# A float32 y split per sub-chunk instead of per piece, and three PSUM banks instead of four for the inner product

## The chip, the cores and the metric

The kernel runs on one core of a Trainium2 chip. The metric is device microseconds (us) of one execution, the median of several. The engines are named as the profile names them: PE (matrix engine, with PEld for its weight loads), DVE (vector), ACT (scalar), POOL (GpSimd) and SP (which issues the DMAs).

## The reference, cut to what matters

```python
X = np.fft.rfft(x, axis=1)                 # x: 8 batches x 3136 tokens x 256
y = np.fft.irfft(X * F, n=3136, axis=1)    # F: complex filter, 1569 bins x 256
h = np.maximum(y @ w_in, 0.0)              # w_in: 256 x 1024
conv = sum(conv_w[k] * hp[:, k:k+3136] for k in range(3))   # hp: h padded by one token at both ends
out = (h * sigmoid(conv)) @ w_out          # w_out: 1024 x 256
```

## The kernel before, in words

**Two phases.** The first (up to about 374 us of the span) does the Fourier transform, the filter and most of the way back for all eight batches, through scratch tensors in device memory. The last stage of the way back is left to be done later, in 14 *pieces* per batch: `last_load` fetches 112x2x256 numbers (`br`), `last_stage` multiplies them by a table into one PSUM bank (eight PE rows of L216 in the trace), and `last_out` writes the result into y. The pieces of batch 0 are done at the end of the first phase, those of batches 1 to 7 inside the second.

**Matrix products in three parts.** `mm3` multiplies float32 numbers as two reduced ones: a rounded part (type fp32r, "hi") and the rest ("lo"); hi x hi, hi x lo and lo x hi are added up in PSUM (L177, L178, L179). So each moving operand must first be split: one copy makes hi, one subtraction makes lo. Before the change y is split as it is written: `last_out` has ACT write hi (`hi_act`, L146) and then DVE write lo (`lo_dve`, L149). y thus exists as two tiles of 3138 tokens a batch, for an even and an odd batch.

**The second phase** goes through 448 *steps* m. A step is one (j, f, i): j is a chunk of 896 tokens (28 of them, 16 steps each), f one of 8 groups of 128 hidden channels, i one of the two sub-chunks of 448 tokens. The program writes the work out in software-pipelined order, and each engine runs its instructions in that order. In step m:

- PE: `inner(m)` (six matmuls of 450 columns into a PSUM tile `ps_h`), the matmuls of a piece if the step has one, then `project(m-6)` (12 matmuls of 256 columns for even steps, 9 for odd ones, into the four banks `po`).
- ACT: `relu(m-1)` (L442, in place in PSUM), a scaled copy to the tile t (L444), the sigmoid of `gate(m-2)` (L454), hi of `split_g(m-3)` (L146, tile g).
- DVE: `conv(m-1)` (L449, L450: two taps from `ps_h` added to t), the product of `gate(m-2)` (L455, called mul(m-2) below; it is the last reader of that step's `ps_h`).
- POOL: lo of `split_g(m-3)` (L152).
- After that `last_out` of the step's piece (ACT, then DVE), and at the end of a chunk, in steps 4 and 5 modulo 16, `evacuate`: two DVE copies each (L490) from `po` to the tile `ot`.

The eight PSUM banks of the second phase are four for `ps_h`, shared by `inner` and the pieces, and four for `po`. The steps with m modulo 16 from 3 to 7 get no piece (`AVOID`). The pieces of a batch are spread over the steps in which the y tiles of the batch two before are no longer read: in some stretches every second or third step has one, and then about 16 steps have none.

Of the kernel before, what the change touches and what calls it, by code (L numbers as in the profile page):

```python
# [22 lines left out]
KT = D // 128  # L23
NF = FF // 128
SUB = 448
NSUB = S // SUB
CH = 2 * SUB
NT = CH // 128


def _k1(g, s):
# [93 lines left out]
def tile_fft_filter_gated_ffn(  # L125
# [16 lines left out]
    nc = tc.nc  # L142
    B = x.shape[0]

    def hi_act(dst, src):
        nc.scalar.activation(dst, src, AF.Copy)  # L146

    def lo_dve(dst, src, hi):
        nc.vector.tensor_tensor(out=dst, in0=src, in1=hi.bitcast(F32), op=ALU.subtract)  # L149

    def lo_pool(dst, src, hi):
        nc.gpsimd.tensor_tensor(out=dst, in0=src, in1=hi.bitcast(F32), op=ALU.subtract)  # L152

# [22 lines left out]
    def mm3(ps, wh, wl, rh, rl, start=True, stop=True, **kw):  # L176
        nc.tensor.matmul(ps, lhsT=wh, rhs=rh, start=start, stop=False, **kw)  # L177
        nc.tensor.matmul(ps, lhsT=wh, rhs=rl, start=False, stop=False, **kw)  # L178
        nc.tensor.matmul(ps, lhsT=wl, rhs=rh, start=False, stop=stop, **kw)  # L179
# [4 lines left out]

    wc = ctx.enter_context(tc.tile_pool(name="wc", bufs=1))
    m2_sb = wc.tile([112, N1], F32, name="m2_sb")
    cw = wc.tile([128, 3, NF], F32, name="cw")
    nc.gpsimd.memset(cw[:, 0, 0:1], 0.0)
    nc.scalar.activation(cw[:, 0, 0:1], cw[:, 0, 0:1], AF.Sigmoid)
    wi = [wc.tile([128, KT, FF], F32R, name=f"wi{h}") for h in range(2)]  # L190
# [3 lines left out]
    ys, yps = {}, []  # L194
# [6 lines left out]

    def y_slices(b, sl):
        if sl.start == 0:
            ys[b] = [yps[b % 2].tile([128, KT, S + 2], F32R, name=f"y{h}") for h in range(2)]
            for t in ys[b]:
                nc.gpsimd.memset(t[:, :, 0:1].bitcast(F32), 0.0)
                nc.gpsimd.memset(t[:, :, S + 1:S + 2].bitcast(F32), 0.0)
        return (t[:, :, 1:S + 1].rearrange("p k (a c) -> p k c a", c=N2)[:, :, sl] for t in ys[b])

    def last_stage(b, c, ps):  # L210

        br = lasts[b, c]
        for j in range(2):
            for k in range(KT):
                o = ps[:, (2 * k + j) * N1:(2 * k + j + 1) * N1]
                nc.tensor.matmul(o, lhsT=br[:, j, 128 * k:128 * k + 128], rhs=m2_sb, start=True, stop=True)  # L216
        lasts[b, c] = ps

    def last_out(b, c):
        yh, yl = y_slices(b, slice(c, c + 2))  # L220
        pv = lasts.pop((b, c))[:, 0:4 * N1].rearrange("p (k c a) -> p k c a", c=2, a=N1)
        hi_act(yh, pv)
        lo_dve(yl, pv, yh)

    forward_pools = ExitStack()
    xp = forward_pools.enter_context(tc.tile_pool(name="xp", bufs=2, side="right"))
# [1 line left out]
    with (  # L228
# [125 lines left out]
        def at(i):  # L354
            return divmod(i, NP) if 0 <= i < NP * B else None
# [12 lines left out]
        with tc.manual_schedule(engines=COMPUTE):  # L368
            for i in range(NI):
                f, m = i, i - SKEW  # L370
                if i == done:
                    for _ in wsteps:
                        pass
                    forward_pools.close()
                    yps.append(ctx.enter_context(tc.tile_pool(name="y_even", bufs=1, side="right", reuse_waits="tile")))
                    lp = ctx.enter_context(tc.tile_pool(name="lp", bufs=2, side="right", reuse_waits="tile"))
                if 1 <= i < 4:
                    nc.sync.dma_start(out=s1_sb[:, 4 * i + 12:4 * i + 16], in_=s1[:, 4 * i + 12:4 * i + 16])
                if (bp := at(f + 7)) and i:
                    load("x", *bp)  # L380
                if bp := at(m + 3):
                    load("a", *bp)
                if i == 6:
                    nc.sync.dma_start(out=s2_sb, in_=s2[:, 0:120])
                    nc.sync.dma_start(out=s2s_sb, in_=s2s[:, 0:120])
                    nc.sync.dma_start(out=m2_sb, in_=m2)
                if 12 <= i < 26 and i % 2 == 0:
                    sl = slice((i - 12) // 2 * 4, (i - 12) // 2 * 4 + 4)
                    load_filter(i // 2 - 6)
                    nc.sync.dma_start(out=i1_sb[:, sl], in_=i1[:, sl])  # L390
                if bp := at(m - 2):
                    filt(*bp)
                pt = third(*bp) if (bp := at(m - 4)) else None
                pf = first(*bp) if (bp := at(f - 1)) else None
                if bp := at(m - 1):
                    second(*bp)
                if pt is not None:
                    store("sb", *at(m - 4), pt)
                if pf is not None:
                    store("sa", *at(f - 1), pf)  # L400
                if 3 <= i < 16:
                    next(csteps, None)
                if i == 16:
                    load_weights(0)
                    load_weights(1)
                if i >= 22:
                    next(wsteps, None)
                if 16 <= i < 30 and i % 2 == 0:
                    copy_filter(i // 2 - 8)
                c = 2 * (i - done)  # L410
                if 0 <= c - 4 < N2:
                    last_out(0, c - 4)
                if 0 <= c - 2 < N2:
                    last_stage(0, c - 2, fps.tile([128, 512], F32, name="ps"))
                if 0 <= c < N2:
                    last_load(0, c)


    yps.append(ctx.enter_context(tc.tile_pool(name="y_odd", bufs=1, reuse_waits="tile")))
    wp = ctx.enter_context(tc.tile_pool(name="wp", bufs=2, reuse_waits="tile"))  # L420
    ps_h = ctx.enter_context(tc.tile_pool(name="ps_h", bufs=4, space=bass.MemoryType.PSUM, reuse_waits="tile"))
    ps_o = ctx.enter_context(tc.tile_pool(name="ps_o", bufs=1, space=bass.MemoryType.PSUM, reuse_waits="tile"))

    outv = out.rearrange("b s d -> (b s) d").rearrange("(j t p) d -> j p t d", p=128, t=NT)
    hs, ts, gs, pos = {}, {}, {}, {}

    def at(m):

        return (m // 16, m // 2 % NF, m % 2) if 0 <= m < 16 * (B * S // CH) else None

    def inner(j, f, i):
        ps = ps_h.tile([128, 512], F32, name="ps_h")[:, 0:SUB + 2]
        fs = slice(128 * f, 128 * f + 128)
        b, u = divmod(2 * j + i, NSUB)
        us = slice(u * SUB, u * SUB + SUB + 2)
        for k in range(KT):
            mm3(ps, wi[0][:, k, fs], wi[1][:, k, fs], ys[b][0][:, k, us], ys[b][1][:, k, us], start=k == 0, stop=k == KT - 1)
        hs[j, f, i] = ps

    def relu(j, f, i):  # L440
# [24 lines left out]
    def project(j, f, i):  # L465
        gh, gl = gs[j, f]
        if f == 0 and i == 0:
            pos[j] = [ps_o.tile([128, 512], F32, name=f"po{k}") for k in range(4)], wp.tile([128, NT, D], F32, name="ot")
        po, ot = pos[j]
        tiles = range(4) if i == 0 else range(4, NT)  # L470
        for t in tiles:
# [7 lines left out]
    def evacuate(j, f, i):  # L479
# [16 lines left out]
    NH = 16 * (B * S // CH)  # L496
    pieces = {}
    for b in range(1, B):
        start = ((NSUB * (b - 1) - 1) // 2 + 1) * 16 + (4 if b == 1 else 0)
        stop = NSUB * b // 2 * 16 + NSUB * b % 2  # L500
        free = [m for m in range(start, stop) if m % 16 not in AVOID]
        for c in range(N2 // 2):
            pieces[free[c * (len(free) - 1) // (N2 // 2 - 1)]] = (b, 2 * c)
    with tc.manual_schedule(engines=COMPUTE):
        for m in range(NH + PLAG):
            if m + 4 in pieces:
                last_load(*pieces[m + 4])
            if a := at(m):
                inner(*a)
            if m in pieces:  # L510
                last_stage(*pieces[m], ps_h.tile([128, 512], F32, name="ps_h"))
            if a := at(m - PLAG):
                project(*a)
            if a := at(m - 1):
                relu(*a)
                conv(*a)
            if a := at(m - 2):
                gate(*a)
            if a := at(m - 3):
                split_g(*a)  # L520
            if m in pieces:
                last_out(*pieces[m])
            if a := at(m - PLAG):
                evacuate(*a)

# [43 lines left out]
```

## Time and profile before

| | us |
|---|---|
| median of 3 runs (1563.34 to 1571.38) | 1569.97 |
| the profiled execution | 1563.82 |
| its span | 1562.0 |
| PE / DVE / ACT / POOL busy | 1503.0 / 1280.6 / 1189.7 / 697.6 |
| second phase, 380 to 1549 us: PE / DVE / ACT / POOL busy of 1169.0 | 1163.4 / 997.8 / 1016.6 / 513.9 |

The profiled execution took 1.8 us more than its span, and 6.2 us less than the median. A row of the timeline gives start, duration, engine, source line, output<-inputs, count, and in brackets the idle time before it with what ended it. A row of groups gives the count, then busy us and mean ns of one, then the idle time before it. Matmul rows overlap, so the time between two starts tells how fast PE goes, not the duration.

### The profile page before, as it was taken

To read this page: it belongs to the slowest core of one execution; us is meant where nothing else is said; L and a number is where in the kernel's file an instruction comes from. 1 tells how busy PE (TensorE), PEld (TensorE's weight loads), DVE (VectorE), ACT (ScalarE), POOL (GpSimd) and SP (SyncE) were. 2 spreads that over 40 slices of the span, in tenths; PEclk is the share of its full clock that TensorE was granted. 3 is DMA by queue.
4 is the path that set the end of the run, shared out by engine and by line. 5 is a ranking of instruction groups with operands and counts; after the bars stand their busy time and mean duration, and the time that the engine had idled before them with its cause. 6 is when DMAs were issued, how large, how long until landed. Compare 5 with 4: busy or idle time off the path is not lost.

```text
span 1562.0 us, 26357 instructions
## 1 busy us (share of the span) xinstructions
PE 1503.0 (96%) x9424; PEld 1346.7 (86%) x9424; DVE 1280.6 (82%) x1965; ACT 1189.7 (76%) x2162; POOL 697.6 (45%) x624
## 2 busy tenths in 40 slices
PE   5799989998999999999999999999999999999998
PEld 3466656656999999999999999999999999999998
DVE  0578888888888888888888888888888888888887
ACT  3444444436888888888888888888888888888887
POOL 0356555643444444444444444444444444444444
PEclk9799999999999999999999999999999999999999
DMA  9999999993111011111110111111011110100001
GB/s 306 298 342 350 330 339 343 335 280 105 31 54 48 31 48 48 48 48 48 48 42 28 33 55 48 48 48 48 31 42 48 48 53 25 48 25 25 25 25 48
DMA packets 129397, 166.82 MB, mean 107 GB/s; under 512 B 10906, under 2 KB 87795, under 8 KB 129267
## 3 DMA queue, kind: packets, MB, share of 16 engines
q1 hardware_dynamic: 129267, 165.14, 32.8%
q8 instruction: 75, 1.23, 0.3%
q14 instruction: 55, 0.45, 0.1%
HBM read 88.03 MB, written 77.07 MB: 106 GB/s over the span
## 4 chain that ended last, share of the span: by engine, by line
PE 82%; DMA 12%; DVE 2%; SPq 1%; ACT 1%; issue 1%; POOL 0%; ACTq 0%; POOLq 0%
PE ps_h L178 12%; PE ps_h L179 12%; PE ps_h L177 11%; PE po L475 11%; PE po L477 11%; PE po L476 11%; PE ps_h L216 6%; DMA a<-a_dram 4%; DMA a_dram<-sa 3%; PE pp L328 3%; PE ps L351 2%; PE ps L321 2%; DMA b_dram<-sb 2%; DVE y L149 1%; ACT y L146 1%
## 5 line engine op out<-in xcount | busy, mean ns | idle before, releaser
L152 POOL TENSOR_TENSOR g<-t,g 128x448 fp32r<-128x448 f32 x448 | 517.5, 1155 | 668.2 <-ACT g L146 266.5
L475 PE MATMUL po<-wo,g 128*128 128x256 f32 x1568 | 441.5, 282 | 0.0
L477 PE MATMUL po<-wo,g 128*128 128x256 f32 x1568 | 433.8, 277 | 0.0
L476 PE MATMUL po<-wo,g 128*128 128x256 f32 x1568 | 433.4, 276 | 0.0
L449 DVE SCALAR_TENSOR_TENSOR t<-ps_h,cw,t 128x448 f32<-128x448 f32 x448 | 305.5, 682 | 82.8 <-ACT t L444 71.9
L178 PE MATMUL ps_h<-y,wi 128*128 128x450 f32 x896 | 330.4, 369 | 4.6 <-DVE y L149 4.6
L177 PE MATMUL ps_h<-y,wi 128*128 128x450 f32 x896 | 328.5, 367 | 3.2 <-DVE t L455 1.5
L179 PE MATMUL ps_h<-y,wi 128*128 128x450 f32 x896 | 328.6, 367 | 0.0
L450 DVE SCALAR_TENSOR_TENSOR t<-ps_h,cw,t 128x448 f32<-128x448 f32 x448 | 306.4, 684 | 16.0
L444 ACT ACTIVATE t<-ps_h,cw 128x448 f32<-128x448 f32 x448 | 285.1, 636 | 41.8 <-POOL g L152 0.4
L475 PEld LDWEIGHTS po<-wo,g 128*128 128x128 f32 x1568 | 294.7, 188 | 7.0
L476 PEld LDWEIGHTS po<-wo,g 128*128 128x128 f32 x1568 | 294.3, 188 | 5.7
L477 PEld LDWEIGHTS po<-wo,g 128*128 128x128 f32 x1568 | 294.4, 188 | 0.0
L442 ACT ACTIVATE ps_h<-ps_h 128x450 f32<-128x450 f32 x448 | 251.7, 562 | 31.8 <-PE ps_h L179 27.2
L455 DVE TENSOR_TENSOR t<-ps_h,t 128x448 f32<-128x448 f32 x448 | 275.1, 614 | 0.1
L454 ACT ACTIVATE t<-t 128x448 f32<-128x448 f32 x448 | 255.0, 569 | 12.1 <-DVE t L450 10.9
L146 ACT ACTIVATE g<-t 128x448 fp32r<-128x448 f32 x448 | 254.4, 568 | 0.2 <-DVE t L455 0.2
L344 POOL TENSOR_TENSOR z<-u,v 120x512 f32<-120x512 f32 x112 | 156.8, 1400 | 172.3 <-DVE v L342 162.9
L309 ACT ACTIVATE sb<-ps 112x512 f32<-112x512 f32 x112 | 66.8, 597 | 159.2 <-DMA b_dram<-sb 87.9
L179 PEld LDWEIGHTS ps_h<-y,wi 128*128 128x128 f32 x896 | 168.3, 188 | 13.9
L178 PEld LDWEIGHTS ps_h<-y,wi 128*128 128x128 f32 x896 | 168.3, 188 | 13.6 <-DVE y L149 6.8
L177 PEld LDWEIGHTS ps_h<-y,wi 128*128 128x128 f32 x896 | 169.9, 190 | 11.5 <-DVE t L455 2.6
(51 smaller groups left out, 1474.0 us busy)
## 6 DMA issues: line engine op xcount, KB each, us to landing
x<-in_x SPq DMA_DIRECT2D x112, 224.0 KB, 4.8
a_dram<-sa SPq DMA_DIRECT2D x112, 224.0 KB, 4.5
a<-a_dram SPq DMA_DIRECT2D x112, 224.0 KB, 4.7
b_dram<-sb SPq DMA_DIRECT2D x112, 224.0 KB, 4.5
br<-b_dram SPq DMA_DIRECT2D x112, 224.0 KB, 2.6
out<-ot SPq DMA_DIRECT2D x27, 896.0 KB, 4.1
raw<-in_w_in SPq DMA_DIRECT2D x8, 256.0 KB, 4.6
raw<-in_w_out SPq DMA_DIRECT2D x8, 256.0 KB, 5.6
```

Of the source, the lines that this page charges most:

```text
L146: nc.scalar.activation(dst, src, AF.Copy)
L152: nc.gpsimd.tensor_tensor(out=dst, in0=src, in1=hi.bitcast(F32), op=ALU.subtract)
L177: nc.tensor.matmul(ps, lhsT=wh, rhs=rh, start=start, stop=False, **kw)
L178: nc.tensor.matmul(ps, lhsT=wh, rhs=rl, start=False, stop=False, **kw)
L179: nc.tensor.matmul(ps, lhsT=wl, rhs=rh, start=False, stop=stop, **kw)
L444: nc.scalar.activation(t, h[:, 1:SUB + 1], AF.Copy, scale=cw[:, 1, f:f + 1])
L449: nc.vector.scalar_tensor_tensor(out=t, in0=h[:, 0:SUB], scalar=cw[:, 0, f:f + 1], in1=t, op0=ALU.mult, op1=ALU.add)
L450: nc.vector.scalar_tensor_tensor(out=t, in0=h[:, 2:SUB + 2], scalar=cw[:, 2, f:f + 1], in1=t, op0=ALU.mult, op1=ALU.add)
L455: nc.vector.tensor_mul(t, h[:, 1:SUB + 1], t)
L475: nc.tensor.matmul(o, lhsT=gh[:, sl], rhs=wo[0][:, f], start=first, stop=False, skip_group_check=True)
L476: nc.tensor.matmul(o, lhsT=gh[:, sl], rhs=wo[1][:, f], start=False, stop=False, skip_group_check=True)
L477: nc.tensor.matmul(o, lhsT=gl[:, sl], rhs=wo[0][:, f], start=False, stop=last, skip_group_check=True)
```

## The change

y is kept once, in float32, in a tile `y` for an even and one for an odd batch. `last_out` becomes a single copy: ACT for batch 0, DVE for the others. A new function `window(n)` splits the 450 tokens (448 and one at either side) that sub-chunk n needs: ACT writes hi of 2 x 450 numbers in a partition, POOL writes lo, into tiles `yw` of three buffers. Windows 0 and 1 are made ahead of the loop, later ones at the ends of steps 13 and 15 modulo 16. `inner` reads the window. The inner product has three PSUM banks of its own (`ps_h`), the pieces have one (`ps_l`); `po` keeps its four. Since a batch's y is free once its last window has been made, the pieces of each batch start where those of the last one stopped, and end some steps before the batch itself begins. Three sizes are raised: `cw` is cut from a tile of 6 instead of 3 planes, a window's row holds 464 numbers, a row of `y` 3144; with these the tiles that PE reads in the second phase start at multiples of 64 bytes (by adding up the tile sizes), where most started 32 bytes off.

```diff
-        hi_act(yh, pv)
-        lo_dve(yl, pv, yh)
+        if engine == "act":
+            nc.scalar.activation(y, pv, AF.Copy)
+        else:
+            nc.vector.tensor_copy(y, pv)
...
-    cw = wc.tile([128, 3, NF], F32, name="cw")
+    cw = wc.tile([128, 6, NF], F32, name="cw")[:, 0:3]
...
+    yw = ctx.enter_context(tc.tile_pool(name="yw", bufs=3, reuse_waits="tile"))
-    ps_h = ctx.enter_context(tc.tile_pool(name="ps_h", bufs=4, space=bass.MemoryType.PSUM, reuse_waits="tile"))
+    ps_h = ctx.enter_context(tc.tile_pool(name="ps_h", bufs=3, space=bass.MemoryType.PSUM, reuse_waits="tile"))
+    ps_l = ctx.enter_context(tc.tile_pool(name="ps_l", bufs=1, space=bass.MemoryType.PSUM, reuse_waits="tile"))
...
+    def window(n):
+        b, u = divmod(n, NSUB)
+        src = ys[b][:, :, u * SUB:u * SUB + SUB + 2]
+        wh, wl = (yw.tile([128, KT, WROW], F32R, name=f"yw{h}")[:, :, 0:SUB + 2] for h in range(2))
+        hi_act(wh, src)
+        lo_pool(wl, src, wh)
+        wins[n] = wh, wl
...
-        start = ((NSUB * (b - 1) - 1) // 2 + 1) * 16 + (4 if b == 1 else 0)
-        stop = NSUB * b // 2 * 16 + NSUB * b % 2
+        start = stop if b > 1 else 4
+        stop = NSUB * b // 2 * 16 - 3 + 2 * (NSUB * b % 2)
...
+        for n in range(2):
+            window(n)
...
             if m in pieces:
-                last_out(*pieces[m])
+                last_out(*pieces[m], "dve")
+            if m % 16 in (13, 15):
+                window(2 * (m // 16 + 1) + (m % 16 == 15))
```

On ACT, before, the queue from the end of step 188 to the end of step 190 (both have a piece; L146 with the output y is the hi copy of a piece, L442 the relu, L444 the scaled copy, L454 the sigmoid, L146 with the output g the hi copy of `split_g`):

```order
L146 ACTIVATE y_8470<-ps_h 128x2x2x112
L442 ACTIVATE ps_h<-ps_h 128x450
L444 ACTIVATE t<-ps_h,cw 128x448
L454 ACTIVATE t<-t 128x448
L146 ACTIVATE g_8870<-t 128x448
L442 ACTIVATE ps_h<-ps_h 128x450
L444 ACTIVATE t<-ps_h,cw 128x448
L454 ACTIVATE t<-t 128x448
L146 ACTIVATE g_8870<-t 128x448
L146 ACTIVATE y_8470<-ps_h 128x2x2x112
```

On ACT, after the change, the queue from the end of step 189 to the end of step 191 (the lines have new numbers: L454 is the relu, L456 the scaled copy, L466 the sigmoid, L148 the hi copy):

```order
L148 ACTIVATE yw_8923<-y 128x2x450
L454 ACTIVATE ps_h<-ps_h 128x450
L456 ACTIVATE t<-ps_h,cw 128x448
L466 ACTIVATE t<-t 128x448
L148 ACTIVATE g_8919<-t 128x448
L454 ACTIVATE ps_h<-ps_h 128x450
L456 ACTIVATE t<-ps_h,cw 128x448
L466 ACTIVATE t<-t 128x448
L148 ACTIVATE g_8985<-t 128x448
L148 ACTIVATE yw_8990<-y 128x2x450
```

The pieces are gone from ACT's queue; two window copies, of twice the elements, stand in it per chunk, each ahead of the next step's relu.

On DVE, before, a step with a piece (185) between two without (L449 and L450 are the taps, L455 the product, L149 the lo of the piece):

```order
L449 SCALAR_TENSOR_TENSOR t<-ps_h,cw,t 128x448
L450 SCALAR_TENSOR_TENSOR t<-ps_h,cw,t 128x448
L455 TENSOR_TENSOR t<-ps_h,t 128x448
L149 TENSOR_TENSOR y_8471<-ps_h,y_8470 128x2x2x112
L449 SCALAR_TENSOR_TENSOR t<-ps_h,cw,t 128x448
```

On DVE, after, from step 180 on (L461 and L462 are the taps, L467 the product, L502 the copies of `evacuate`):

```order
L502 COPY ot<-po_8207 128x512
L502 COPY ot<-po_8208 128x512
L461 SCALAR_TENSOR_TENSOR t<-ps_h,cw,t 128x448
L462 SCALAR_TENSOR_TENSOR t<-ps_h,cw,t 128x448
L467 TENSOR_TENSOR t<-ps_h,t 128x448
L502 COPY ot<-po_8209 128x512
L502 COPY ot<-po_8210 128x256
L461 SCALAR_TENSOR_TENSOR t<-ps_h,cw,t 128x448
```

The copies of `evacuate` stand where they stood before, ahead of the taps of the next step; in a step with a piece, one copy (L223) stands where L149 stood. PE's queue keeps its order within a step. What changes there is the wait ahead of `inner(m)`: before, it waits for mul(m-4) in 251 of the steps, for mul(m-3) in 98 and for a piece's L149 in 91; after, for mul(m-3) in all 445 from step 3 on.

More of the change, by code (lines that the diff above doesn't have):

```diff
@@ L28 @@
 NT = CH // 128
+WROW = 464
+YROW = 3144
 def _k1(g, s):
@@ L146, in hi_act @@
         nc.scalar.activation(dst, src, AF.Copy)
-    def lo_dve(dst, src, hi):
-        nc.vector.tensor_tensor(out=dst, in0=src, in1=hi.bitcast(F32), op=ALU.subtract)
     def lo_pool(dst, src, hi):
@@ L203, in y_slices @@
         if sl.start == 0:
[L204 to L208, printed above, removed]
+            ys[b] = t = yps[b % 2].tile([128, KT, YROW], F32, name="y")
+            nc.gpsimd.memset(t[:, :, 0:1], 0.0)
+            nc.gpsimd.memset(t[:, :, S + 1:S + 2], 0.0)
+        return ys[b][:, :, 1:S + 1].rearrange("p k (a c) -> p k c a", c=N2)[:, :, sl]
     def last_stage(b, c, ps):
@@ L217, in last_stage, with last_out @@
         lasts[b, c] = ps
-    def last_out(b, c):
-        yh, yl = y_slices(b, slice(c, c + 2))
+    def last_out(b, c, engine):
+        y = y_slices(b, slice(c, c + 2))
         pv = lasts.pop((b, c))[:, 0:4 * N1].rearrange("p (k c a) -> p k c a", c=2, a=N1)
-        hi_act(yh, pv)
-        lo_dve(yl, pv, yh)
+        if engine == "act":
+            nc.scalar.activation(y, pv, AF.Copy)
+        else:
+            nc.vector.tensor_copy(y, pv)
     forward_pools = ExitStack()
@@ L411, in tile_fft_filter_gated_ffn @@
                 if 0 <= c - 4 < N2:
-                    last_out(0, c - 4)
+                    last_out(0, c - 4, "act")
                 if 0 <= c - 2 < N2:
@@ L419, in tile_fft_filter_gated_ffn @@
     yps.append(ctx.enter_context(tc.tile_pool(name="y_odd", bufs=1, reuse_waits="tile")))
+    yw = ctx.enter_context(tc.tile_pool(name="yw", bufs=3, reuse_waits="tile"))
     wp = ctx.enter_context(tc.tile_pool(name="wp", bufs=2, reuse_waits="tile"))
-    ps_h = ctx.enter_context(tc.tile_pool(name="ps_h", bufs=4, space=bass.MemoryType.PSUM, reuse_waits="tile"))
+    ps_h = ctx.enter_context(tc.tile_pool(name="ps_h", bufs=3, space=bass.MemoryType.PSUM, reuse_waits="tile"))
+    ps_l = ctx.enter_context(tc.tile_pool(name="ps_l", bufs=1, space=bass.MemoryType.PSUM, reuse_waits="tile"))
     ps_o = ctx.enter_context(tc.tile_pool(name="ps_o", bufs=1, space=bass.MemoryType.PSUM, reuse_waits="tile"))
     outv = out.rearrange("b s d -> (b s) d").rearrange("(j t p) d -> j p t d", p=128, t=NT)
-    hs, ts, gs, pos = {}, {}, {}, {}
+    hs, ts, gs, pos, wins = {}, {}, {}, {}, {}
     def at(m):
         return (m // 16, m // 2 % NF, m % 2) if 0 <= m < 16 * (B * S // CH) else None
+    def window(n):
+        if n >= B * NSUB:
+            return
+        b, u = divmod(n, NSUB)
[4 more added lines that the diff above has]
+        wins[n] = wh, wl
     def inner(j, f, i):
@@ L433, in inner @@
         fs = slice(128 * f, 128 * f + 128)
-        b, u = divmod(2 * j + i, NSUB)
-        us = slice(u * SUB, u * SUB + SUB + 2)
+        wh, wl = wins[2 * j + i]
         for k in range(KT):
-            mm3(ps, wi[0][:, k, fs], wi[1][:, k, fs], ys[b][0][:, k, us], ys[b][1][:, k, us], start=k == 0, stop=k == KT - 1)
+            mm3(ps, wi[0][:, k, fs], wi[1][:, k, fs], wh[:, k], wl[:, k], start=k == 0, stop=k == KT - 1)
         hs[j, f, i] = ps
@@ L510, in tile_fft_filter_gated_ffn @@
             if m in pieces:
-                last_stage(*pieces[m], ps_h.tile([128, 512], F32, name="ps_h"))
+                last_stage(*pieces[m], ps_l.tile([128, 512], F32, name="ps_l"))
             if a := at(m - PLAG):
```

## The prediction

> **What bounds the kernel now.** I read the page first (busy times, granted clock), then the windows by stage, the groups by line, and last the timeline of the steps around an `evacuate`.
>
> ```profile
> PE 1503.0 (96%) x9424; PEld 1346.7 (86%) x9424; DVE 1280.6 (82%) x1965; ACT 1189.7 (76%) x2162; POOL 697.6 (45%) x624
> PEclk9799999999999999999999999999999999999999
> PE 82%; DMA 12%; DVE 2%; SPq 1%; ACT 1%; issue 1%; POOL 0%; ACTq 0%; POOLq 0%
> 380.00:1549.00 1169.00, 1163.40 (x8083) 1116.39 (x8082) 997.76 (x1542) 1016.55 (x1879) 513.93 (x472) 1.00 0.13 41
> PE ps_h L178 <- DVE y L149: 3.9, 7, 0.6
> PE ps_h L177 <- DVE t L455: 1.5, 3, 0.8
> ```
>
> The third row is the chain that ended last, PE's for 82% of the span. The fourth is a window (busy us of PE, PEld, DVE, ACT, POOL, then clock), the last two are waits from 380 us on (us in all, times, longest). In the second phase PE hardly rests: 5.6 of 1169.0 us are gaps, and its only waits are seven for the split of a new batch's y and three at the start. No work is taken from PE by this change, so it can gain only these few us, something in the first phase, or a faster matmul stream. It can lose wherever PE is made to wait. So the question is how much slack lies between PE and the engines that give its PSUM banks back.
>
> ```profile
> L450 DVE SCALAR_TENSOR_TENSOR t<-ps_h,cw,t 128x448 f32<-128x448 f32 x448 | 306.4, 684 | 16.0
> L444 ACT ACTIVATE t<-ps_h,cw 128x448 f32<-128x448 f32 x448 | 285.1, 636 | 41.8 <-POOL g L152 0.4 <-ACT ps_h L442 0.4
> L146 ACT ACTIVATE y<-ps_h 128x448 fp32r<-128x448 f32 x98 | 103.9, 1060 | 71.7 <-PE ps_h L216 71.7
> L149 DVE TENSOR_TENSOR y<-ps_h,y 128x448 fp32r<-128x448 f32 x98 | 103.2, 1053 | 76.9 <-ACT y L146 76.9
> L490 DVE COPY ot<-po 128x512 f32<-128x512 f32 x83 | 54.2, 679 | 3.2 <-PE po L477 3.2
> L253 ACT ACTIVATE t_sb<-t_sb 56x1024 f32<-56x1024 f32 x7 | 7.4, 1055 | 0.2
> L152 POOL TENSOR_TENSOR g<-t,g 128x448 fp32r<-128x448 f32 x448 | 517.5, 1155 | 668.2 <-ACT g L146 266.5 <-issue 243.8 <-POOL g L152 83.9
> ```
>
> An undisturbed step, and then one chunk's steps 6 and 7 (406 and 407 by count), which follow the four copies of `evacuate`. Each PE row is the first matmul of an `inner`, each L455 the product that frees a bank:
>
> ```profile
> 1460.61 0.61 DVE L455 TENSOR_TENSOR t<-ps_h,t 128x448 f32<-128x448 f32 x1
> 1461.40 0.37 PE L177 MATMUL ps_h<-y,wi 128*128 128x450 f32 x1
> ...
> 1446.64 1.28 DVE L490 COPY ot<-po 128x512 f32<-128x512 f32 x2
> 1449.14 0.61 DVE L455 TENSOR_TENSOR t<-ps_h,t 128x448 f32<-128x448 f32 x1
> 1449.15 0.37 PE L177 MATMUL ps_h<-y,wi 128*128 128x450 f32 x1
> 1449.67 1.01 DVE L490 COPY ot<-po 128x512 f32<-128x512 f32 x2
> 1451.74 0.37 PE L177 MATMUL ps_h<-y,wi 128*128 128x450 f32 x1
> 1451.91 0.61 DVE L455 TENSOR_TENSOR t<-ps_h,t 128x448 f32<-128x448 f32 x1
> 1453.76 0.61 DVE L455 TENSOR_TENSOR t<-ps_h,t 128x448 f32<-128x448 f32 x1
> 1453.98 0.37 PE L177 MATMUL ps_h<-y,wi 128*128 128x450 f32 x1
> ```
>
> Undisturbed, mul(m-3) ends at 1461.22 and `inner(m)` starts at 1461.40: 0.18 us to spare. After the copies it is otherwise: mul(403) ends at 1449.75, 0.60 after `inner(406)` has begun; mul(404) at 1452.52, 0.78 after `inner(407)`. Four banks allow this. Three do not. And DVE can hardly be quicker: behind the end of an `inner` come the relu, L444 (636 ns), two taps (684 each), and only then, in the order of its queue, the product of the step before, some 3.3 us, where two steps of PE (1449.15 to 1453.98) take 4.83.
>
> **The change, part by part.** The sum goes against the profiled execution's 1563.8.
>
> *A. Three banks at the evacuation: +22.7.* In the first steps of the phase four banks already bind, and show how soon PE follows a product:
>
> ```profile
> 381.29 0.61 DVE L455 TENSOR_TENSOR t<-ps_h,t 128x448 f32<-128x448 f32 x1
> 381.96 0.47 PE L177 MATMUL ps_h<-y,wi 128*128 128x450 f32 x1 [0.79 <-DVE t L455]
> ```
>
> The product ends at 381.90, PE starts 0.06 later. With mul(m-3) awaited everywhere, `inner(406)` starts at 1449.75 + 0.06 instead of 1449.15: 0.66 late. `inner(407)`, then due at 1452.40, must wait for 1452.58: 0.18 more, 0.84 in all. `inner(408)`, due at 1454.82, finds mul(405) done at 1454.37 and waits no more. DVE runs without a gap through these rows, so a later PE hardly moves them: the relu of step 406 comes 0.66 later, and its taps are then ready about when DVE gets to them. Behind the waiting `inner`, in PE's queue, stands only the `project` of its step, which is then as late; its g and its banks are ready. 27 chunks have an evacuation inside the loop: 27 x 0.84 = 22.7. Lower end 15 (if half of the second wait and some of the first are taken up), upper 31 (1.16 each, if the lag that steps with pieces now leave behind stays).
>
> *B. Windows on ACT: +3.9.* A window's hi is 900 elements; by L253 (1024 in 1055 ns) and the L146 below (448 in 0.57) about 0.95 us. The idle time of ACT into which it falls, ahead of the next step's relu, is 0.40:
>
> ```profile
> 1457.03 0.57 ACT L146 ACTIVATE g<-t 128x448 fp32r<-128x448 f32 x1
> 1457.99 0.53 ACT L442 ACTIVATE ps_h<-ps_h 128x450 f32<-128x450 f32 x1 [0.40 <-PE ps_h L179]
> ```
>
> So the relu, and with it the product and the bank, comes 0.55 later; 0.18 - 0.06 = 0.12 of that is spare, 0.43 is PE's wait. Where a piece stands in the same or a neighbouring step, PE has some 0.9 us of other work and the delay is hidden. By the table of pieces that leaves 9 of the 54 windows: 3.9. Were no delay hidden: 23. POOL takes at most 2 x 1.155 = 2.3 us for a window's lo, and is idle more than half of each step; `project` uses the g behind it two steps later, so nothing waits. The first use of a window, too, is two or three steps behind it.
>
> *C. The start of the second phase: +4.5.*
>
> ```profile
> 371.08 2.61 ACT L146 ACTIVATE y<-ps 128x448 fp32r<-128x448 f32 x3
> 372.10 2.73 DVE L149 TENSOR_TENSOR y<-ps,y 128x448 fp32r<-128x448 f32 x3 [2.06 <-ACT y L146]
> 373.74 0.47 PE L177 MATMUL ps_h<-y,wi 128*128 128x450 f32 x1 [1.47 <-ACT y L146]
> 374.88 0.74 PE L178 MATMUL ps_h<-y,wi 128*128 128x450 f32 x1 [0.67 <-DVE y L149]
> 375.42 0.58 PE L179 MATMUL ps_h<-y,wi 128*128 128x450 f32 x1
> 375.80 0.58 PE L177 MATMUL ps_h<-y,wi 128*128 128x450 f32 x1
> ```
>
> Now the second matmul comes 1.19 us after the last copy of y (373.69). Then ACT (0.95) and POOL (up to 2.3) stand between: 3.3, or 2.1 later; the second window, whose POOL part queues behind the first, costs 1.2 against now. I take 2. And the fourth bank, which lets PE run ahead in the first steps (the wait at 381.96 above would come one step earlier), is worth 1.3 to 2.9; I take 2.5.
>
> The matmuls at 375.42 and 375.80 stand 0.38 apart, against 0.20 later in the phase: after the gaps PE runs at half rate for a while. The Trainium skill (TensorE: Matmul & The Clock Gate, section "What's actually happening") has windows of about 3.4 us, an idle one of which halves the clock; a longer pause here could by that rule cost one more such window, an estimated 1.7 us, and the sum would be 1590. These starts agree that there is such a stretch now; no run here shows a second.
>
> *D. The seven waits for a new batch's y: -4.* The row "PE ps_h L178 <- DVE y L149" has 3.9 us; the last piece now ends at least one whole step ahead of the window that reads it. The fetches of `br` move with the pieces, four steps ahead as before on a DMA share of 0.13, and POOL's two small memsets of a new y stand ahead of nothing that is awaited: 0.
>
> *E. The last pieces of the first phase: -3.*
>
> ```profile
> 336.70:370.30 33.60, 30.56 (x164) 23.37 (x165) 30.17 (x40) 16.53 (x22) 13.69 (x15) 1.00 0.71 212
> L149 DVE TENSOR_TENSOR y<-ps,y 128x448 fp32r<-128x448 f32 x14 | 13.8, 1002 | 4.6 <-ACT y L146 4.2
> ```
>
> In this stretch DVE is busy 30.2 of 33.6 us, PE 30.6. Eleven of DVE's L149 fall into it; without them DVE needs 19, and PE is next: at most 33.6 - 30.6 = 3.0 are won. Ends 0 and 6 (if PE's matmul rows include waiting).
>
> *F. Placement of the tiles: 0.* Nothing in the trace compares a 64-byte boundary with another for all of a matmul's operands. What it has:
>
> ```profile
> 1452.35 0.36 PE L177 MATMUL ps_h<-y,wi 128*128 128x450 f32 x1
> 1452.96 0.28 PE L475 MATMUL po<-wo,g 128*128 128x256 f32 x1
> ```
>
> The three matmuls from 1451.74 and the three from 1452.35 read rows of y that lie 12,552 bytes apart, 8 off from one another modulo 64, and both triples take 0.61. So I take 0. Per column, `inner` takes 1.22 / (6 x 450) = 0.452 ns (1451.74 to 1452.96) and `project` 1.02 / (9 x 256) = 0.443 (from there to 1453.98); `inner` at the rate of `project` would give 2688 x 450 x 0.009 ns = -11 us, the nearest end.
>
> *G. DVE's copy for a piece: 0.* Its write has the same stride as L149 and L146 (both about 1.05), so between 0.61 (L490 by elements) and 1.05. It need not wait for ACT as L149 does (76.9 us in all). It delays the next taps by up to 0.8, against PE's 0.9 for the piece, so the bank is still in time; without a piece's PE time there would be no such copy.
>
> Sum: 22.7 + 3.9 + 4.5 - 4 - 3 = +24.1, so **1588**. The median of the runs before is 6.2 above the profiled one; I leave the number between the two ways of counting.
>
> **Rivals.**
>
> *R1, faster: the matmul stream speeds up with aligned operands.* Speaks for it: 0.452 ns a column in `inner` is not the least that PE shows, since a float32 matmul of 512 columns starts its second row about 0.42 us after its first, 0.41 ns for half a float32 column:
>
> ```profile
> 329.72 1.02 PE L328 MATMUL pp<-a,s_sb 112*120 112x512 f32 x2
> ```
>
> (1.02 less the last one's 0.6). At 0.41, `inner` saves 19 ns a matmul, 51 us in all; what `project` saved beyond that would be lost again, as the way of the bank described above would then be longer than PE's two steps. Against it: F's equal triples. Taken at two thirds of the way from nothing to -51, with 2 back for longer waits in A: 1588 - 34 + 2 = **1556**. It decides from 9 ns a matmul on (24.1 / 2688). The Trainium skill (TensorE: Matmul & The Clock Gate, section "Wait — 56ns, not 53.3ns?") measures N / 2.4 GHz + 2.5 ns between matmuls, 190 for 450 columns, and by it the sum would be an estimated 1553; the trace has 203, and no run here shows 190.
>
> *R2, slower still: delays add up.* Windows are hidden by no piece (+19 over B) and the evacuation costs 1.16 (+8): **1615**. For it: 0.12 us is all the slack there is, and POOL, DVE and ACT get new neighbours. Against it: pieces stand beside 45 of the 54 windows.
>
> *R3, no difference: three banks do not bind as I read it.* If the stall of A is taken up in part by an earlier DVE (the waits for ACT in L149's row are gone) and E gives its 6: 1563.8 + 11 + 4 + 4 - 4 - 6 = **1573**, within 0.5% of 1570. Against it: chunks without any piece show the same 0.60 and 0.78.
>
> **How the numbers follow.** Forecast 0.44, R1 0.22, R2 0.17, R3 0.17. The forecast's own range is 1577 to 1601 (A from 15 to 31, C and E by their ends). Eight in ten: down to 1550, which leaves out the lower part of R1, up to 1610, which leaves out the upper half of R2. About 0.5% (8 us) is what a measurement of this kernel can tell from no change. Slower by more: most of the forecast and R2, 0.61; within: R3 and the edges of the forecast and R1, 0.17; faster: most of R1, 0.22.
>
> **What would show it.** Right: in the profile after, PE waits for the product (L467) some 27 times or more, 20 to 30 us in all, most in steps 6 and 7 of a chunk; no wait for y at the start of a batch; steps without a piece still 2.25 and 2.59 us. Wrong: starts of `inner`'s matmuls closer than 0.20 (R1), PE's waits for the product also in steps 15 and 1 (R2), or PE as gapless as before (R3).

## Result and the profile after

The changed kernel takes 1593.41 us (median, 1592.34 to 1594.2), the kernel before, run beside it, 1569.4 (1563.34 to 1571.38). The ratio is 1.0159, 95% interval 1.0131 to 1.0188: slower by 24 us. The profiled execution took 1594.2 with a span of 1592.4, against 1562.0 before. The page of the changed kernel (busy times, granted clock, chain), and one window of the second phase:

```profile
PE 1520.2 (95%) x9424; PEld 1359.5 (85%) x9424; DVE 1246.0 (78%) x1951; ACT 1148.3 (72%) x2120; POOL 812.2 (51%) x664
PEclk9799999998999999999999999999999999999999
PE 64%; DVE 8%; ACT 3%; issue 1%; POOL 0%; ACTq 0%; DVEq 0%
380.00:1580.00 1200.00, 1183.01 (x8094) 1130.53 (x8094) 977.90 (x1545) 975.22 (x1837) 624.54 (x513) 1.00 0.13 40
```

DVE and ACT have less to do than before, and yet PE, which had 5.6 us of gaps in this phase, now has 17.0 (1200.00 - 1183.01), and DVE has a larger share of the chain (8% instead of 2%). The granted clock has an 8 in the tenth slice, where the second phase starts; before it was a 9. What PE waits for, from 396 us on, so without the start of the phase (us in all, times, longest):

```profile
PEld ps_h L176 <- DVE t L467: 19.1, 33, 0.7
PE ps_h L176 <- DVE t L467: 12.5, 27, 0.5
```

27 waits for the product that frees a bank, as many as there are evacuations inside the loop, all of them ahead of the `inner` of a chunk's step 6, and none for a new y. What one of them looks like, in the chunk whose steps 6 and 7 the prediction shows of before (L467 is the product, L502 the copy of `evacuate`, L176 the first matmul of each triple):

```profile
1472.19 0.61 DVE L467 TENSOR_TENSOR t<-ps_h,t 128x448 f32<-128x448 f32 x1
1472.72 1.28 DVE L502 COPY ot<-po 128x512 f32<-128x512 f32 x2
1473.02 0.36 PE L176 MATMUL ps_h<-yw,wi 128*128 128x450 f32 x1
...
1475.23 0.61 DVE L467 TENSOR_TENSOR t<-ps_h,t 128x448 f32<-128x448 f32 x1
1475.76 1.01 DVE L502 COPY ot<-po 128x512 f32<-128x512 f32 x2
1475.90 0.47 PE L176 MATMUL ps_h<-yw,wi 128*128 128x450 f32 x1 [0.46 <-DVE t L467]
1476.20 0.37 PE L177 MATMUL ps_h<-yw,wi 128*128 128x450 f32 x1
...
1478.00 0.61 DVE L467 TENSOR_TENSOR t<-ps_h,t 128x448 f32<-128x448 f32 x1
1478.67 0.48 PE L176 MATMUL ps_h<-yw,wi 128*128 128x450 f32 x1
1480.05 0.61 DVE L467 TENSOR_TENSOR t<-ps_h,t 128x448 f32<-128x448 f32 x1
1481.04 0.37 PE L176 MATMUL ps_h<-yw,wi 128*128 128x450 f32 x1
```

The product of step 403 ends at 1475.84, `inner(406)` starts at 1475.90; the product of step 404 ends at 1478.61, `inner(407)` starts at 1478.67. Both follow by 0.06; the second shows no idle time, since the row's modelled ends of the matmuls ahead cover it. `inner(408)` at 1481.04 waits no more. Step 5 takes 2.88 us (1473.02 to 1475.90) instead of 2.25, step 6 2.77 instead of 2.59, step 7 2.37 instead of 2.25.

From the starts of `inner` the whole second phase can be added up. An undisturbed step of before takes 2.247 us (odd) or 2.587 (even), a piece 0.913. What the steps of chunks 1 to 26 take beyond that:

| steps mod 16 | before | after |
|---|---|---|
| 5, 6, 7 (`evacuate`) | 0.0 | 24.9 |
| 14, 15, 0, 1 (windows; before: a new batch) | 7.0 | 2.9 |
| all others | -0.1 | 2.1 |
| all | 6.9 | 29.9 |

### The profile page after: what moved, and what is told of

It is laid out like the page before. It is cut to its first block, busy times and chain, and to the rows that moved or that the text cites. A ratio compares the mean times of both kernels' runs of the same rounds, so it can differ in the third digit from the quotient of the medians.

```text
span 1592.4 us, 26281 instructions
## 1 busy us (share of the span) xinstructions
PE 1520.2 (95%) x9424; PEld 1359.5 (85%) x9424; DVE 1246.0 (78%) x1951; ACT 1148.3 (72%) x2120; POOL 812.2 (51%) x664
## 4 chain that ended last, share of the span: by engine, by line
PE 64%; DVE 8%; ACT 3%; issue 1%; POOL 0%; ACTq 0%; DVEq 0%
PE ps_h L176 11%; PE ps_h L178 10%; PE ps_h L177 10%; PE po L487 9%; PE po L488 9%; PE po L489 9%; PE ps_l L214 5%; DVE t L461 2%; DVE t L467 2%; DVE ot L502 2%; DVE t L462 1%; ACT t L456 1%; ACT ps_h L454 1%; ACT yw L148 0%; POOL yw L151 0%
## 5 line engine op out<-in xcount | busy, mean ns | idle before, releaser
L461 DVE SCALAR_TENSOR_TENSOR t<-ps_h,cw,t 128x448 f32<-128x448 f32 x448 | 302.4, 675 | 206.3 <-ACT t L456 203.1
L454 ACT ACTIVATE ps_h<-ps_h 128x450 f32<-128x450 f32 x448 | 237.7, 531 | 187.9 <-PE ps_h L178 178.8
L176 PE MATMUL ps_h<-yw,wi 128*128 128x450 f32 x896 | 336.1, 375 | 19.5 <-DVE t L467 16.8
L177 PE MATMUL ps_h<-yw,wi 128*128 128x450 f32 x896 | 329.7, 368 | 1.4 <-POOL yw L151 1.4
L178 PE MATMUL ps_h<-yw,wi 128*128 128x450 f32 x896 | 331.0, 369 | 0.0
L462 DVE SCALAR_TENSOR_TENSOR t<-ps_h,cw,t 128x448 f32<-128x448 f32 x448 | 306.4, 684 | 16.0
L456 ACT ACTIVATE t<-ps_h,cw 128x448 f32<-128x448 f32 x448 | 284.9, 636 | 41.2
L467 DVE TENSOR_TENSOR t<-ps_h,t 128x448 f32<-128x448 f32 x448 | 275.0, 614 | 0.1
L466 ACT ACTIVATE t<-t 128x448 f32<-128x448 f32 x448 | 254.5, 568 | 0.5 <-DVE t L462 0.5
L148 ACT ACTIVATE g<-t 128x448 fp32r<-128x448 f32 x448 | 254.0, 567 | 0.2 <-DVE t L467 0.2
L176 PEld LDWEIGHTS ps_h<-yw,wi 128*128 128x128 f32 x896 | 170.0, 190 | 37.4 <-DVE t L467 25.0
L178 PEld LDWEIGHTS ps_h<-yw,wi 128*128 128x128 f32 x896 | 169.6, 189 | 12.9
L177 PEld LDWEIGHTS ps_h<-yw,wi 128*128 128x128 f32 x896 | 169.5, 189 | 9.4 <-POOL yw L151 1.9
```

What stands on the lines that cost most here:

```text
L456: nc.scalar.activation(t, h[:, 1:SUB + 1], AF.Copy, scale=cw[:, 1, f:f + 1])
L461: nc.vector.scalar_tensor_tensor(out=t, in0=h[:, 0:SUB], scalar=cw[:, 0, f:f + 1], in1=t, op0=ALU.mult, op1=ALU.add)
L462: nc.vector.scalar_tensor_tensor(out=t, in0=h[:, 2:SUB + 2], scalar=cw[:, 2, f:f + 1], in1=t, op0=ALU.mult, op1=ALU.add)
L466: nc.scalar.activation(t, t, AF.Sigmoid)
L467: nc.vector.tensor_mul(t, h[:, 1:SUB + 1], t)
```

## Experiments

Of each, the time is the median, the ratio that to the kernel before on the same chip, with its 95% interval.

| | time | ratio |
|---|---|---|
| changed kernel | 1593.4 | 1.0159 (1.0131 to 1.0188) |
| e1 four shared banks | 1560.5 | 0.9967 (0.9953 to 0.998) |
| e2 before, with three and one | 1679.6 | 1.0727 (1.0701 to 1.0753) |
| e3 no padding | 1598.0 | 1.0213 (1.0189 to 1.0236) |
| e4 `evacuate` on two engines | 1573.2 | 1.0034 (1.0019 to 1.005) |
| e5 e1, moved by 32 bytes | 1562.4 | 0.9982 (0.9971 to 0.9994) |
| e6 e1, another start | 1558.5 | 0.9955 (0.994 to 0.997) |
| e7 pieces copied by ACT | 1694.4 | 1.0827 (1.0807 to 1.0847) |
| e8 e5 and e6 | 1561.1 | 0.9976 (0.9964 to 0.9988) |
| e9 before, pieces earlier | 1558.9 | 0.996 (0.9947 to 0.9974) |

**e1: four shared banks.**

```diff
-    ps_h = ...tile_pool(name="ps_h", bufs=3, ...)
-    ps_l = ...tile_pool(name="ps_l", bufs=1, ...)
+    ps_h = ...tile_pool(name="ps_h", bufs=4, ...)
-                last_stage(*pieces[m], ps_l.tile(...))
+                last_stage(*pieces[m], ps_h.tile(...))
```

> The changed kernel, with its pieces back in one ring of four PSUM banks that the inner products and the last stage share; y kept once, the windows and all else stay. Theory (the lost bank is the cost): in the trace of the changed kernel, chunks 1 to 26, the steps 5, 6 and 7 of a chunk are 0.637, 0.182 and 0.137 us longer than before, 0.956 a chunk, 25.8 us over 27 chunks; steps 14, 15, 0 and 1, next to the windows, some 2 us in all; the first eight steps 6.1. With four banks the first two go and about 4 of the third: 1593 - 25.8 - 2 - 4 = 1562, with steps 5 and 6 back at 2.25 and 2.59 us, at or a little below the time before. Rival W (the windows' own copies on ACT and POOL make inner late, whatever the banks): at most the evacuation's part returns in steps without a window, and the time stays above 1580. Rival P (placement of the tiles made the matmul stream slower): 1590, all of the loss stays.

1560.5. One window of the second phase, and the steps that follow an evacuation (L466 is the product, L501 the copy here):

```profile
380.00:1545.00 1165.00, 1163.51 (x8074) 1121.15 (x8073) 972.83 (x1540) 976.82 (x1833) 623.26 (x511) 1.00 0.13 41
1444.12 1.28 DVE L501 COPY ot<-po 128x512 f32<-128x512 f32 x2
1444.41 0.36 PE L176 MATMUL ps_h<-yw,wi 128*128 128x450 f32 x1
1446.62 0.61 DVE L466 TENSOR_TENSOR t<-ps_h,t 128x448 f32<-128x448 f32 x1
1446.67 0.37 PE L176 MATMUL ps_h<-yw,wi 128*128 128x450 f32 x1
```

PE's gaps are 1.5 of 1165 us. `inner(406)` starts at 1446.67 while the product of step 403 is still to run until 1447.23, as it did before. Steps 5, 6 and 7 have nothing left but what all steps have here (0.013 us each where there is no piece), and steps 14, 15, 0 and 1 neither. So the windows on ACT and POOL cost nothing of their own in the steady state: rival W falls. What is lost lies in the bank.

**e2: the kernel before, with three banks and one.**

```diff
-    ps_h = ...tile_pool(name="ps_h", bufs=4, ...)
+    ps_h = ...tile_pool(name="ps_h", bufs=3, ...)
+    ps_l = ...tile_pool(name="ps_l", bufs=1, ...)
-                last_stage(*pieces[m], ps_h.tile(...))
+                last_stage(*pieces[m], ps_l.tile(...))
```

> The kernel before, with one edit: three banks for the inner products and one for the pieces' last stage. No window exists in it, and no tile is padded. Theory: the evacuation costs 27 x 0.96 = 25.8, the first steps of the second phase some 3, so at least 1598; steps with a piece, where ACT spends 1.06 us on y's hi ahead of the next relu against 0.91 us of PE's work for the piece, may add up to 0.15 each, 15 in all: 1598 to 1613, steps 5 to 7 long as in the changed kernel. Rival W: without windows three banks are enough, 1570. Rival P: 1570.

Steps 5, 6 and 7 cost 0.925 us a chunk, as expected, in a kernel that has none of the other edits. But the time is 1680, 67 above the upper end. The rest lies in the steps next to a piece, some 0.84 us for each (the 7.0 of a new batch taken off). Around step 33 (L146 ACT's hi of y, L443 the relu, L456 the product):

```profile
475.34 1.04 PE L216 MATMUL ps_l<-m_sb,br 112*128 112x112 f32 x8
475.44 0.61 DVE L456 TENSOR_TENSOR t<-ps_h,t 128x448 f32<-128x448 f32 x1
476.42 1.05 ACT L146 ACTIVATE y<-ps_l 128x448 fp32r<-128x448 f32 x1 [1.40 <-PE ps_l L216]
477.24 0.67 ACT L443 ACTIVATE ps_h<-ps_h 128x450 f32<-128x450 f32 x1
477.50 1.05 DVE L149 TENSOR_TENSOR y<-ps_l,y 128x448 fp32r<-128x448 f32 x1 [1.45 <-ACT y L146]
```

The matmuls of the step's `inner` stand ahead of the piece's (475.34); its relu starts only at 477.24, since ACT first waits 1.40 us for the piece and then copies it. I had counted the copy (1.06) against PE's time for the piece (0.91) and left out that ACT waits for it in order. Two things could be meant by that, ACT's order or DVE's wait for ACT's hi; e7 tells them apart.

**e3: no padding.**

```diff
-WROW = 464
-YROW = 3144
+WROW = SUB + 2
+YROW = S + 2
-    cw = wc.tile([128, 6, NF], F32, name="cw")[:, 0:3]
+    cw = wc.tile([128, 3, NF], F32, name="cw")
```

> The changed kernel with the padding of its tiles undone (rows of 450 and 3138 elements, cw of three rows); banks, windows and order stay. Theory: the waits at the banks stay, and the time is 1593; of the 13 ns that steps without a piece are longer than before (some 4 us over the phase, from the first three matmuls of a project at 119 to 124 ns instead of 113) some may go: 1589 to 1594. Rival P: the padding is what made it slower, 1570. Rival R1 of the prediction (aligned operands speed the stream up): the padding hides a part of the loss, over 1600, with starts of inner's matmuls farther apart than 203 to 205 ns.

1598.0, 4 above the range: the loss at steps 5 to 7 stays (23.7 us in the 26 chunks, against 24.9), and the other steps are longer; from `inner(8)` to the last `inner` it takes 1187.6 us instead of 1181.8. So the padding is not what made the kernel slower; it makes it 5.8 us faster. It is not `inner` that is slower (its matmuls start 203.3 ns apart on average, 204.7 in the changed kernel) but `project`: of its matmuls 78 in 100 start 116 to 118 ns after the one ahead. In the changed kernel 70 in 100 have 112 to 114, and most of the first ones of a step 116 to 124. The kernel before had 112 to 114 for 92 in 100; the expectation of e5 says every one, which is too much.

**e4: `evacuate` on two engines.** DVE keeps the copies of even number; ACT makes the others one step later, behind its hi of g.

```diff
+            if not end and k % 2 != late:
+                continue
-            if end and k % 2:
+            if k % 2:
                 nc.scalar.activation(o, src, AF.Copy)
...
                 evacuate(*a)
+            if a := at(m - PLAG - 1):
+                evacuate(*a, late=1)
```

> The changed kernel with its three banks; of a chunk's four copies of evacuate, DVE keeps the two of even number, in the steps where they are, and ACT makes the two of odd number one step later, behind its hi of g. Theory (the cost is the time for which evacuate keeps DVE from the product that frees the bank): DVE's block is 0.64 us in each of two steps instead of 1.28 and 1.01, the product of step 403 then ends before inner(406) is due, and ACT's 0.60 falls into an idle time of 0.42, which delays the next product by some 0.1: 27 x (0.96 - 0.1) = 23 us come back, 1570 (1566 to 1580). Rival W: the windows set the loss, 1585 to 1593. Rival P: 1593.

```profile
1450.35 0.68 DVE L504 COPY ot<-po 128x512 f32<-128x512 f32 x1
1450.64 0.36 PE L176 MATMUL ps_h<-yw,wi 128*128 128x450 f32 x1
1451.55 0.59 ACT L502 ACTIVATE ot<-po 128x512 f32<-128x512 f32 x1
1452.25 0.61 DVE L467 TENSOR_TENSOR t<-ps_h,t 128x448 f32<-128x448 f32 x1
1452.92 0.47 PE L176 MATMUL ps_h<-yw,wi 128*128 128x450 f32 x1
```

1573.2, 20 us back with three banks. One copy (0.68) now stands ahead of the product of step 403, which ends at 1452.86 instead of some 0.6 later; `inner(406)` follows 0.06 behind it, 2.28 after `inner(405)`. Steps 5, 6 and 7 cost 0.16 a chunk instead of 0.92. So the price is the time for which `evacuate` keeps DVE.

**e5: e1 moved by 32 bytes.**

```diff
-    cw = wc.tile([128, 6, NF], F32, name="cw")[:, 0:3]
+    cw = wc.tile([128, 3, NF], F32, name="cw")
```

> The kernel with the shared ring of four banks, with cw back at three rows, which moves every later tile by 32 bytes: all operands of the matmuls, weights, windows and g, then stand 32 past a 64-byte boundary instead of on it; their distances from one another stay. So far: in the kernel before (weights, g and t at 32) every project matmul starts 113 to 114 ns after the one ahead; in the changed kernel (all at 0) 113 to 114 but 119 to 124 for the first ones of a step; in the kernel without padding (weights at 32, g and t at 0, windows at both) 116 to 118 for nearly all. Theory D (the distance between the operands counts, not the boundary): the same time, within 2 us of the shared ring's 1560.5. Rival 32 (a place at 32 is the good one, as in the kernel before): steps without a piece go from 2.260 and 2.600 to 2.247 and 2.587 us, 4 to 6 us less, 1555. Rival 0 (the boundary counts, as the change takes it): slower by 5 to 9 us, 1566 to 1570.

1562.4; the phase from `inner(8)` takes 1156.4 instead of 1154.6 us, and the first matmuls of a `project` still start 119 to 124 ns apart. Neither rival: moving all tiles off the 64-byte boundary together changes next to nothing (1.8 us), where e3, in which their distances differ, cost 5.8. What sets the 119 to 124 stays open.

**e6: e1, another start.** Of the last pieces of the first phase DVE copies two, and DVE makes window 0's lo.

```diff
-                    last_out(0, c - 4, "act")
+                    last_out(0, c - 4, "dve" if c - 4 in (20, 24) else "act")
...
-        lo_pool(wl, src, wh)
+        (lo_pool if n else lo_dve)(wl, src, wh)
```

> The kernel with the shared ring of four banks, with another start of the second phase: of the last four copies of y in the first phase DVE, idle there, makes two, and DVE makes window 0's lo instead of POOL. In the traces the last copies on ACT stand in a row (three in 2.61 us), POOL needs 2.08 for a window's lo, and the second matmul of inner(0) waits for it. Theory: y is done about 0.9 us sooner, window 0's lo about 1 us after its hi instead of 2.1, window 1's lo, no longer behind it on POOL, 1 us sooner: 2 to 3 us, 1558. Rival (the start is set by the granted clock, which stays at half for a time after the pause whatever ends it): below 1 us, 1560.

```profile
369.06 1.10 DVE L151 TENSOR_TENSOR yw<-y,yw 128x900 fp32r<-128x900 f32 x1 [1.95 <-ACT yw L148]
369.07 0.47 PE L179 MATMUL ps_h<-yw,wi 128*128 128x450 f32 x1 [2.10 <-ACT yw L148]
370.21 0.74 PE L180 MATMUL ps_h<-yw,wi 128*128 128x450 f32 x1 [0.66 <-DVE yw L151]
```

1558.5, the lowest median of all, though its interval overlaps those of e1 and e9. The second matmul comes 1.14 us after the first instead of 2.16, and from the end of the first phase's last copy to `inner(8)` it takes 20.1 us instead of 22.1 in e1. The granted clock is 0.50 for 3.4 us here (369.8 to 373.2) and for 6.8 in e1 (372.8 to 379.7), so the rival, the clock, is not ruled out for a part of the 2 us. e8, this with the move by 32 bytes, adds the two (20.5 us there, 1156.5 in the phase):

> Shared ring of four banks, the other start of the second phase and the move by 32 bytes, all three. Theory: the two edits add: 1560.5 - 2.5 + 0 = 1558, and 1553 if rival 32 holds, 1564 if rival 0 holds. It is faster than the kernel before by 0.5% or more unless rival 0 holds.

1561.1, 3 above what was expected of it (e5 was 2 above), and faster than before by 0.24%, not by the 0.5%.

**e7: pieces copied by ACT.**

```diff
-                last_out(*pieces[m], "dve")
+                last_out(*pieces[m], "act")
```

> The changed kernel (three banks and one) with one word changed: in the second phase the copy of a piece to y is made by ACT instead of DVE. The kernel before with three banks and one took 1680 us, 80 more than was expected of it; its steps 5, 6 and 7 cost the expected 0.925 us a chunk, and the rest lies in the steps next to a piece. Theory (ACT's order is the cause: its copy waits for the piece's last stage, 1.4 us, takes 1.05, and the next step's relu stands behind it; three banks have no room for that): each of the 98 pieces costs about 0.8 us, 1593 + 80 = 1673 (1650 to 1685). Rival (in that kernel DVE's lo of y, which waits for ACT's hi and holds the taps behind it, was the cause): DVE is free of pieces here, so the time stays at 1593 or falls, up to 1605.

```profile
PEld ps_h L176 <- DVE t L467: 115.2, 133, 2.0
ACT y L221 <- PE ps_l L214: 103.0, 98, 1.4
PE ps_h L176 <- DVE t L467: 87.8, 123, 1.6
```

1694.4: 101 us for 98 pieces, 1.03 each, 9 above the range. ACT's 98 copies wait 103 us for the piece's matmuls, with the next relu behind them; DVE no longer waits for an ACT copy of a piece here, so its wait can't be the cause. ACT's order is, and by itself it costs no less than the 0.84 of e2.

**e9: before, pieces earlier.**

```diff
-        stop = NSUB * b // 2 * 16 + NSUB * b % 2
+        stop = NSUB * b // 2 * 16 - 3 + 2 * (NSUB * b % 2)
```

> The kernel before with one line changed: the last piece of each batch stands two to four steps ahead of the first step that reads the new y, as in the changed kernel, instead of one; y, its split and the shared ring stay. Theory: in the trace of before, the seven chunks in which a batch begins are some 0.9 us longer than the rest, 6.9 us over the phase where steps 15, 0 and 1 stand above 2.25 and 2.59; all of it goes, 1565.6 - 6.9 = 1559, a ratio of 0.9956, so that this one line brings what the shared ring of four with its windows brings (0.9967). Rival (only the 3.9 us that the prediction read from the row of waits go): 1562, a ratio of 0.9975. Rival (the wait moves to another place): 1566.

1558.9, and the steps of chunks 1 to 26 take 0.1 us less than their undisturbed times in all, where the kernel before had 6.9 more. So one line of the change is worth 7.0 us by the steps (6.0 by the medians), and in the median it alone gives what e1 gives with all the rest (the two intervals overlap).

## Why the prediction was right

The time forecast was 1588, against 1593.4; the mechanism was the forecast's own. Its terms, with what the traces measured:

| | forecast | measured |
|---|---|---|
| A, bank at the evacuation | +22.7 | +24.8 |
| B, windows on ACT | +3.9 | +2.4 |
| C, start of the phase | +4.5 | +7.1 |
| D, waits for a new y | -4 | -7.0 |
| E, last pieces of the first phase | -3 | -4.5 |
| F, placement | 0 | +4 |
| G, DVE's copy for a piece | 0 | 0 |
| sum | +24.1 | +26.8 |

The two profiled spans differ by 30.4; 3.8 of that lies in the first phase ahead of its last pieces, where nothing was changed. Its 98th copy of the way back ends between 330.1 and 335.2 us in the eleven profiles of this case, at 330.6 before and at 334.4 after: scatter from one execution to the next. The medians differ by 24.0.

That the sum came so close is in part luck. A, C and F came out 2.1, 2.6 and 4 above their terms, B, D and E 1.5, 3.0 and 1.5 below, and these errors cancel but for 2.7. Of the signs named ahead, the 27 waits came, and no wait for a new y. "20 to 30 us in all, most in steps 6 and 7" did not come as a row of waits: the row has 12.5 us, all ahead of step 6. The starts of `inner` show the loss: 24.9 us in steps 5, 6 and 7.

- **A** was right in place and mechanism, shown from three sides: four banks take it away (e1), three banks bring the same 0.925 us a chunk into the kernel before (e2), and half the block on DVE takes most of it away (e4). It is 0.92 a chunk instead of 0.84. Less the 0.013 that all steps have, step 5 is 0.62 longer (forecast 0.66) and step 6 0.17 (0.18); what was missing are 0.12 in step 7. A matmul behind a wait costs more than the wait: from 1475.90 the next start follows after 0.30 us instead of 0.20, and likewise at 1478.67.
- **B**: 2.9 us in steps 14, 15, 0 and 1, of which 0.7 stand there in e1 too; 2.4 over all chunks. e1 has the same windows and none of it, so it, too, is a price of three banks. Step by step against e1, it lies behind the windows of steps 77, 189, 301, 397, 399, 413, 415, 429 and 431 and behind no other. These are the nine that have a piece neither in their own step nor in a neighbouring one, the forecast's count; each costs 0.27 instead of 0.43.
- **C** was too small. From the end of the last copy of the first phase (`sb`) to `inner(8)` it takes 19.4 us before, 22.1 in e1, 26.5 after: 2.6 for the windows (forecast 2), 4.5 for the bank (forecast 2.5), each with a share of the clock in it. The bank's part:

```profile
376.25 0.74 PE L177 MATMUL ps_h<-yw,wi 128*128 128x450 f32 x1 [1.43 <-POOL yw L151]
379.76 0.68 DVE L461 SCALAR_TENSOR_TENSOR t<-ps_h,cw,t 128x448 f32<-128x448 f32 x1 [13.03 <-ACT t L456]
383.09 0.61 DVE L467 TENSOR_TENSOR t<-ps_h,t 128x448 f32<-128x448 f32 x1
383.75 0.48 PE L176 MATMUL ps_h<-yw,wi 128*128 128x450 f32 x1 [2.03 <-DVE t L467]
```

  `inner(3)` waits 2.03 us for the first product, one step sooner than before. Behind these waits the granted clock falls a second time. Four windows, of PE, PEld, DVE, ACT and POOL, with the clock as the third number from the end:

```profile
374.00:380.00 6.00, 4.49 (x11) 3.63 (x12) 0.24 (x1) 2.03 (x4) 4.16 (x2) 0.50 0.02 5
380.00:390.00 10.00, 6.22 (x26) 4.42 (x25) 8.07 (x14) 7.81 (x15) 2.68 (x3) 1.00 0.00 0
390.00:394.00 4.00, 3.41 (x13) 3.14 (x13) 2.45 (x5) 2.74 (x6) 1.88 (x2) 0.57 0.00 0
394.00:404.00 10.00, 10.00 (x71) 9.63 (x71) 7.17 (x12) 7.62 (x15) 3.53 (x5) 1.00 0.08 25
```

  The clock is 0.50 until 380 us, 1.00, then 0.57 around 392, and 1.00 to the end. In e4 and e7, whose first steps have nearly the same waits, it stays at 1.00 there, and from `inner(6)` to `inner(8)` they need 5.1 us, this kernel 6.4: 1.3 us of C are this second stretch. The first stretch, too, is longer than before: 6.8 us (373.2 to 380.1) instead of 3.4 (374.4 to 377.8). e4 has 3.4 there too, and needs 24.8 us in all instead of 26.5. So some 1.8 us of C are the clock, an estimate from these two traces, and 5.4 the windows and the bank, against a forecast of 4.5. The forecast had priced one more stretch at an estimated 1.7 us and left it out of its sum. The Trainium skill (TensorE: Matmul & The Clock Gate, section "What's actually happening") says that the window over which PE's activity is judged runs freely and does not start with the work. These traces are consistent with that, though they do not show the window: nearly the same waits, with the second stretch in one kernel and without it in the two others.

- **D** was too small: I took the 3.9 us of idle time from the row of waits, where the steps show 7.0 (e9). The idle time that the trace gives a matmul is not all that PE loses. In the kernel before, `inner(49)` starts at 502.85 us: the second matmul starts 0.95 us after the first instead of 0.20, and the third 0.31 after the second: 0.86 late in all. The row has 0.56 there, since it counts from the modelled end of the first matmul (0.39 after its start). A shows the same, 12.5 us of idle time in 27 waits against 24.8 lost.
- **E** was right in sign and within its ends, though more than the 3.0 that it called the most: from the 98th copy of the way back to the last one it takes 40.3 to 40.6 us in the three kernels that split y as it is written, 35.7 to 37.0 in the eight others.
- **F**: taken as 0. In the changed kernel `project` takes 0.013 us more in a step without a piece, 4 in all; that the placement is what costs it is not shown, since e5 leaves open what sets the 119 to 124. With the new tiles and without the padding it would have been 5.8 more (e3). R1, the aligned stream, doesn't show: `inner`'s matmuls start 204.7 ns apart on average, 205.1 before.
- **G** was right only because DVE makes the copy. e7 prices the other choice at 101 us. The prediction's reason is that the copy on DVE "need not wait for ACT". What e7 prices is another one: ACT no longer waits for the piece, with the relu behind it. I did not see that.

R2 (1615) had the evacuation at 1.16 and no window hidden: neither came. R3 fell with the 27 waits.

## What to carry to other kernels

Count a ring of buffers by the longest time from one use to the release that the slowest engine's order allows, not by its mean: here three banks suffice in most steps, and the block of two copies on DVE makes the others late, 25 us in all. A copy that waits for another engine holds whatever stands behind it in its own engine's order, and whether this costs anything is decided by the slack of the ring further on: with four banks the piece's copy on ACT was free, with three it cost 0.84 (e2) to 1.03 us (e7) each. And when a change has several parts, the one that pays may be the smallest: one line that ends the pieces a few steps sooner is worth 7 us here, and e6, which keeps the new y and the windows but gives the fourth bank back, takes 1558.5.

## What was not expected of the hardware

A matmul of `inner` that has waited for its bank is followed by the next after 305 to 317 ns instead of 199 to 211, so that each such wait costs 0.1 us beyond itself. Where tiles lie moves most of `project`'s matmuls of 256 columns from 112 to 114 ns (the changed kernel) to 116 to 118 (e3), 5.8 us in all, while a shift of all of them by 32 bytes (e5) costs 1.8. The granted clock fell to half a second time in the changed kernel, for 3.4 us from 390.3 on, with no wait of PE over 2.03 us in the 10 us ahead of it, and not in e4 and e7 with nearly the same waits.
